# Filling TensorE's waits between attention and the first expert's first product

## The chip, the cores and the metric

The kernel runs on one NeuronCore of a Trainium2 chip. TensorE multiplies, VectorE, ScalarE and GpSimd work on vectors, SyncE (SP) issues most transfers; each engine runs its own instructions in order and waits on semaphores. The time is device microseconds of one execution, given as a median of several; the profile is of one more execution.

## What is computed

Attention over 8 batches, 8 heads, 576 positions and 64 features gives a matrix x of 4608 tokens by 512. Each token then goes to one of eight experts, 576 tokens to each. The reference takes the pairs of token and expert by falling logit, so that the expert that fills first, and with which tokens, comes out of a sorted sweep:

```python
logits = x @ w_gate
order = np.argsort(-logits.flatten())
for idx in order:
    tok, e = (int(idx) // E, int(idx) % E)
    if assigned[tok] >= 0 or counts[e] >= cap:
        continue
    assigned[tok] = e
    counts[e] += 1
for e in range(E):
    mask = assigned == e
    h = np.maximum(x[mask] @ w1[e], 0.0)
    out[mask] = h @ w2[e]
```

## The kernel before

Attention runs in 16 units. A planner (`Plan`) orders each unit's steps on five engines; with the table of due times that the kernel carries, every engine takes its steps in that order. Its PSUM buffers are four, named `g`. The last unit also gives the logits `L`, in the layout of 128 rows by 36 columns of tokens.

Between attention and the experts stands `routing(0)`, the search for the first full expert, written straight in code. A token's best logit is split into six digits. For each digit VectorE compares all tokens with the digit's 32 or 64 values (`cmp`, in pieces), TensorE counts per expert with 36 small products into `rps`, VectorE turns the counts into flags and a sum `da`, one product with `e8s` spreads it, and VectorE takes the digit off (`ch`, `cc`). The first digit's count is mostly made during attention (`part`); what is left of it is 9 products. The first four digits have 32 values and the last two 64 (`fin` is the last). Then come the marks `gt`, a scan and a product with `tri` and `dif` for the rank of each token, two one-hot tables (`hv`, `lo`, the latter compared in three pieces), 18 products, and eight small ones that give the list `idx`: columns 0 to 4 are the rows of the expert's tokens in blocks of 128 (the last of 64), column 5 is an index of half rows, used when the last block is written out.

Idle products, `idle(n)`, of ones with 512 columns into a spare PSUM tile `y1` (PSUM is the accumulator memory), stand at three places: behind the rank product (4), behind `idx` (11), and behind the transposes of the first two blocks (4 and 3).

Tiles of the experts come from a pool `fp`, which takes over SBUF that attention's tiles had. The first instruction of an engine that writes into it waits for all earlier users. `wk` is a one-element copy on GpSimd of a piece of `lo`, in the pool `rt`, which has no earlier users.

The rest of the work is planned as in attention, with a table. What matters here, in the order of each engine for expert 0: GpSimd gathers the five blocks (`xg`), with a copy of the expert's number (`ei`) behind the second one; SP loads the third and fourth piece of the first weight (`raww`) by that copied number; ScalarE splits each weight piece into a high part `w1h`, the residue `w1l` is VectorE's; the gathered blocks are transposed on TensorE into PSUM buffers `h` (four of them) and split the same way into `xh` and `xl`. The products of `xh`, `xl` with the weights (L922) go into the same four buffers; ScalarE's relu gives `fh`, VectorE the residue `fl`, which frees the buffer. ScalarE has the split of the third and fourth weight piece ahead of the first relu. The routing for expert 1 runs in between, on VectorE and TensorE. VectorE's update of the logits for it (L744 to L752) stands behind the last column of `idx`.

Of the kernel before, what the change touches and what calls it, by code (L numbers as in the profile page):

```python
# [97 lines left out]
def attention(ctx, tc, nc, q, k, v, w_phi, w_gate, xs, L, C, xp, cfg={}, after=None, later=None, count=None, init=iter(())):  # L98
# [39 lines left out]
    NG=4  # L138
# [14 lines left out]
    def unit(u):  # L153
# [130 lines left out]
        for g,(j0,j1) in enumerate(JG):  # L284
            n=j1-j0; due=d['num']+d['ns']*g
            js=sorted(set(j//3 for j in range(j0,j1)))
            def pe(x,g=g,j0=j0,j1=j1):
                p=T['np',u,g]=pair(('g',u,'num',g))(x)
                for a in range(2):
                    for j in range(j0,j1):  # L290
                        for fh in range(2):
                            for ab in range(2):
                                PE.matmul(p[64*ab:64*ab+64,a,73*(j-j0):73*(j-j0)+73],T['qP',u,j//3][:,fh,a,ab,j%3,:],T['kz',u][:,a,fh,ab,:],start=fh==0,stop=fh==1)  # L293
            def dve(x,g=g,j0=j0,j1=j1,n=n):
                p=T['np',u,g][:,:,0:73*n].rearrange('p a (j e) -> p a j e',e=73)
                rd=sb.tile([128,2,n,1],F32,name='rd',bufs=2)
                V.tensor_scalar(rd,p[:,:,:,72:73],1e-6,None,op0=OP.add)
                V.reciprocal(rd,rd)
                if g==0: T['x',u]=(xp if lastu else sb).tile([128,9,144],F32,name='xp',bufs=1 if lastu else 2)
                x_=T['x',u]  # L300
                Lb=L[:,9*bp+j0:9*bp+j1,:]
                if lastu:
                    L3=C['L3'][:,j0:j1]
                    for a in range(2): V.tensor_mul(L3[:,:,:,1+a],p[:,a,:,64*a:64*a+8],rd[:,a].to_broadcast([128,n,8]))
                    V.tensor_reduce(Lb.rearrange('p j (e o) -> p j e o',o=1),L3,axis=AX.X,op=OP.add)
                    if g==1: after()
                    for a in range(2):
                        for j in range(n): A.activation(x_[:,j0+j,8+64*a:72+64*a],p[:,a,j,8-8*a:72-8*a],AF.Copy,scale=rd[:,a,j,:])
                else: V.tensor_mul(x_[:,j0:j1].rearrange('p j (a e) -> p a j e',a=2),p[:,:,:,0:72],rd.to_broadcast([128,2,n,72]))
            add(('num',g),'PE',n*515.,due,pe,['zk']+[('ex',j) for j in js],'B',slots(('g',NG,'num',g)),tuple(('qP',u,j) for j in js)+(('kz',u),),ins=32*n)  # L310
            add(('x',g),'DVE',(430+dv(144*n)) if not lastu else 900.,due+2.7,dve,[('num',g)],seq=('x',0) if g else None,slot=slots(('xb',2)) if g==0 else (),frees=(('g',u,'num',g),))
        def st(x):
            for a in range(2):
                o=bass.AP(tensor=xs.tensor,offset=xs.offset+(1152*bp+576*a)*512+128*hp,ap=[[512,64],[64*512,9],[1,128]])
                nc.sync.dma_start(o,T['x',u][64*a:64*a+64,:,8:136])
# [243 lines left out]
def moe(ctx, tc, nc, L, xs, w1, w2, out, C, MC, R0, rt, cfg={}):  # L559
# [18 lines left out]
    def idle(n):  # L578

        p=ps.tile([128,512],F32,name='y1',bufs=1)  # L580
        for _ in range(n): PE.matmul(p,ones,ones[:,None,:].to_broadcast([128,4,128]),start=True,stop=True)
    def routing(r):

        last = r==E-1
        wide = r<cfg.get('wide',1)
        if not last:
# [4 lines left out]
            for i,(sh,bits) in enumerate(DIG):  # L591
                K=KW[i]; n=128//K; fin=i==ND-1
                part='n0' in R and i==0
                if part:
                    p=rps([8,K])
                    cnt0(R,p,NT//9-1,cmp0(R,NT//9-1),True,True)
                else:
                    cmp=S([128,NT//n,K,n],f'cmp{K}',BF,b=2)
                    cv=c.rearrange('p (g i) -> p g i',i=n)
                    g=0  # L600
                    for ck in ((WC if K==32 else WC2) if wide else (9,)*(1 if K==32 else 2)):
                        V.tensor_tensor(cmp[:,g:g+ck],cv[:,g:g+ck,None,:].to_broadcast([128,ck,K,n]),
                                        kt[i].rearrange('p (k i) -> p k i',i=n)[:,None].to_broadcast([128,ck,K,n]),op=OP.is_ge); g+=ck
                if 'rest' in R:
                    with tc.issue_after(R['last']):
                        if i: 
                            for _ in R.pop('rest'): pass
                        else: next(R['rest'])
                yield
                if part: pass  # L610
                elif wide:
                    p=rps([8,K])
                    for t in range(NT):
                        PE.matmul(p,OH[:,t,:],cmp[:,t//n,:,t%n],start=t==0,stop=t==NT-1)
                else:
                    p=rps([128,n,8])
                    for g in range(NT//n):
                        PE.matmul(p,cmp[:,g].rearrange('p k i -> p (k i)'),OH[:,g*n:g*n+n,:],start=g==0,stop=g==NT//n-1)  # L618
                    yield
                    mm=S([128,n,8],f'mm{n}'); V.tensor_mul(mm,p,msk[n])  # L620
                    V.tensor_reduce(tin[:,0:8].rearrange('p (e o) -> p e o',o=1),mm.rearrange('p i e -> p e i'),axis=AX.X,op=OP.add)
                    tr=S([128,32],'tr'); V.transpose(tr,tin)
                    yield
                    cn8=S([128,32//n,1],f'cn{n}'); V.tensor_reduce(cn8,tr.rearrange('p (k i) -> p k i',i=n),axis=AX.X,op=OP.add)
                    f32=S([128,32//n],f'f{n}'); V.tensor_scalar(f32,cn8[:,:,0],float(cap),2.0**(-7*i),op0=OP.is_ge,op1=OP.mult)
                    ds8=S([128,1],'ds'); V.tensor_reduce(ds8,f32,axis=AX.X,op=OP.add)
                if wide:
                    fl=S([8,K],f'fl{K}',BF); da=S([8,1],'da',BF)
                    with nc.allow_low_precision(reason='counts up to 64'):
                        if part: V.scalar_tensor_tensor(fl,p,-float(cap),R['n0'],op0=OP.add,op1=OP.is_ge,accum_out=da)  # L630
                        else: V.tensor_scalar(fl,p,float(cap),0.0,op0=OP.is_ge,op1=OP.add,accum_out=da)
                else:
                    fl=S([128,8],'fl128',BF); V.tensor_scalar(fl,eye8,ds8,None,op0=OP.mult)
                yield
                p=rps([128,8])
                if wide: PE.matmul(p,da.to_broadcast([8,128]),e8s[:,i],start=True,stop=True)
                else: PE.matmul(p,ones,fl,start=True,stop=True)
                if r: yield
                ch=S([128,1],'ch'); V.tensor_reduce(ch,p,axis=AX.X,op=OP.max)
                lat=cfg.get('latd',.7)  # L640
                if fin: break
                c2=S([128,NT],'cc',BF,b=2)
                V.scalar_tensor_tensor(c2,c,ch,dg[:,i+1],op0=OP.subtract,op1=OP.add); c=c2
                if r: yield
# [29 lines left out]
        PE.matmul(p[:,1],dif,gt[:,0],start=False,stop=True)  # L674
        if wide: idle(4)
        if r: yield
# [21 lines left out]
        l2=sf[:,0].rearrange('p (g i) -> p g i',i=2)  # L698
        lk=6 if wide else 9
        for g in range(0,18,lk):  # L700
            V.tensor_tensor(lo[:,g:g+lk],l2[:,g:g+lk,None,:].to_broadcast([128,lk,64,2]),
                            kl.rearrange('p (k i) -> p k i',i=2)[:,None].to_broadcast([128,lk,64,2]),op=OP.is_equal)
        if wide:

            wk=S([1,1],'wk',BF); G.tensor_copy(wk,lo[0:1,0,0,0:1])
        yield
# [5 lines left out]
        if wide:  # L712
# [3 lines left out]
            for j in range(4):  # L716
                for o in (0,64):
                    k=5 if o==0 else 4
                    PE.matmul(p[o:o+64,0:k],dup2[:,j%2,o:o+64],pb[:,o//64:9:2,j//2,j%2],start=j==0,stop=j==3,skip_group_check=True)
            V.tensor_copy(idx[:,0:4,0],p[:,0:4])  # L720
            V.tensor_copy(idx[0:64,4,0:1],p[0:64,4:5])
        else:

# [14 lines left out]
        if not last:  # L738
            yield 'up'
            if wide:  # L740
                p=rps([128,1])
                for j in range(4): PE.matmul(p,dup2[:,j%2],pb[:,8:9,j//2,j%2],start=j==0,stop=j==3)
                V.tensor_scalar(idx[:,5],p,2.0,half,op0=OP.mult,op1=OP.add)
            E1=S([128,8],'E1'); V.tensor_scalar(E1,f8,mx,None,op0=OP.is_equal)  # L744
# [66 lines left out]
    for r in range(E):  # L811
# [132 lines left out]
        for bb,(o,nn) in enumerate(BL):  # L944
# [43 lines left out]
            add(('ys',r,bb),'POOL',1250.,due+d['y']+.5,ys,[('yc',r,bb)],frees=(('ysb',r,bb),)+((('idx',r),) if r else ()),lat=2800.,lock=True)  # L988
    idle(11)
    for x in P.order(): x['fn'](x)  # L990
# [64 lines left out]
```

## Time and profile before

| what | value |
|---|---|
| median of 3 runs | 763.65 us (763.33 to 764.94) |
| the profiled execution | 765.09 us, of which 763.2 us are its span |
| TensorE busy | 736.1 us, 96% of the span |
| VectorE busy | 571.4 us, 75% |
| ScalarE busy | 348.2 us, 46% |
| GpSimd busy | 312.0 us, 41% |
| mean granted TensorE clock | 0.977 of full |

Busy shares are means over stages with different limits, so they do not tell which wait counts; the stretches and timelines below do. In them the first number is the start in us from the beginning of the span. A busy time of several products ends with the tail of the last one. What stands in brackets is the idle time just before on that engine and what ended it. The granted clock is 1.00 at 2.4 GHz and 0.50 at 1.2 GHz.

### The profile page before, as it was taken

To read this page: it belongs to the slowest core of one execution; us is meant where nothing else is said; L and a number is where in the kernel's file an instruction comes from. 1 tells how busy PE (TensorE), PEld (TensorE's weight loads), DVE (VectorE), ACT (ScalarE), POOL (GpSimd) and SP (SyncE) were. 2 spreads that over 40 slices of the span, in tenths; PEclk is the share of its full clock that TensorE was granted. 3 is DMA by queue.
4 is the path that set the end of the run, shared out by engine and by line. 5 is a ranking of instruction groups with operands and counts; after the bars stand their busy time and mean duration, and the time that the engine had idled before them with its cause. 6 is when DMAs were issued, how large, how long until landed. Compare 5 with 4: busy or idle time off the path is not lost.

```text
span 763.2 us, 25319 instructions
## 1 busy us (share of the span) xinstructions
PE 736.1 (96%) x10832; PEld 633.3 (83%) x10832; DVE 571.4 (75%) x1495; ACT 348.2 (46%) x612; POOL 312.0 (41%) x336
## 2 busy tenths in 40 slices
PE   7999999999999966999999999999999999999997
PEld 3888888998898864788897897897897897897985
DVE  5999899989997975996796796796796795673410
ACT  2677677877788431333522422422422422542411
POOL 6797888988889701103103103103103103312002
PEclk9999999999999985999999999999999999999999
DMA  9979688988883032325405405406405406662301
GB/s 168 153 136 154 132 166 165 165 142 156 156 167 81 13 86 75 104 107 186 160 1 182 164 2 183 163 1 186 160 1 184 163 2 198 236 190 60 132 15 49
DMA packets 236944, 94.28 MB, mean 124 GB/s; under 512 B 185904, under 2 KB 223184, under 8 KB 236832
## 3 DMA queue, kind: packets, MB, share of 16 engines
q1 hardware_dynamic: 225552, 71.91, 40.4%
q0 software_dynamic: 6608, 20.16, 8.3%
q8 instruction: 85, 1.39, 0.8%
q10 hardware_dynamic: 4672, 0.59, 0.6%
q14 instruction: 27, 0.22, 0.1%
HBM read 72.58 MB, written 20.05 MB: 121 GB/s over the span
## 4 chain that ended last, share of the span: by engine, by line
PE 65%; issue 13%; DVE 12%; POOL 4%; ACT 2%; SPq 2%; DMA 1%; POOLq 0%; DVEq 0%
PE h L922 22%; PE y L953 18%; PE g L293 8%; DVE kgm L189 4%; PE y L968 3%; PE g L185 3%; PE g L276 2%; PE g L231 2%; SPq L122 2%; DVE qgt L192 2%; DVE qgm L189 2%; PE rps L618 2%; POOL ks L222 1%; PE g L247 1%; PE h L887 1%
## 5 line engine op out<-in xcount | busy, mean ns | idle before, releaser
L983 POOL DMA_INDIRECT out_dram<-ysb,idx x40 | 39.2, 981 | 335.9 <-ACT ysb L976 329.9
L222 POOL TENSOR_TENSOR ks<-ks,kP 128x512 f32<-128x512 f32 x112 | 143.2, 1279 | 7.4 <-ACT kP L213 0.2
L922 PE MATMUL h<-xh,w1l 128*128 128x272 f32 (+3 forms) x512 | 142.0, 297 | 0.3 <-DVE w1l L840 0.2
L922 PE MATMUL h<-xh,w1h 128*128 128x272 f32 (+3 forms) x512 | 141.6, 302 | 0.1
L935 ACT ACTIVATE fh<-h 128x272 fp32r<-128x272 f32 (+2 forms) x128 | 49.1, 384 | 136.6 <-PE h L922 128.8
L953 PE MATMUL y<-w2h,fh 128*128 128x512 f32 x256 | 101.2, 398 | 0.0
L953 PE MATMUL y<-w2l,fh 128*128 128x512 f32 x256 | 99.9, 395 | 0.0
L953 PE MATMUL y<-w2h,fl 128*128 128x512 f32 x256 | 99.3, 392 | 0.0
L922 PEld LDWEIGHTS h<-xh,w1l 128*128 128x128 f32 x512 | 97.1, 190 | 1.8 <-DVE w1l L840 0.8
L922 PEld LDWEIGHTS h<-xh,w1h 128*128 128x128 f32 x512 | 96.0, 190 | 2.0 <-issue 0.4
L922 PE MATMUL h<-xl,w1h 128*128 128x272 f32 (+3 forms) x512 | 93.3, 299 | 1.1 <-DVE xl L897 1.1
L213 ACT ACTIVATE kP<-kgt 128x768 f32<-128x768 f32 x96 | 73.9, 837 | 34.0 <-POOL kgt L201 19.0
L939 DVE SCALAR_TENSOR_TENSOR fl<-h,fh 128x272 fp32r<-128x272 f32 (+2 forms) x128 | 53.0, 416 | 38.7 <-ACT fh L935 22.2
L293 PE MATMUL g<-kz,qP 128*64 128x73 f32 x2304 | 78.9, 229 | 2.0 <-DVE kz L262 1.8
L293 PEld LDWEIGHTS g<-kz,qP 128*64 128x64 f32 x2304 | 76.3, 138 | 3.8 <-DVE kz L262 1.9
L280 ACT ACTIVATE qP<-g 128x768 f32<-128x768 f32 x96 | 70.9, 813 | 16.1 <-PE g L276 16.1
L922 PEld LDWEIGHTS h<-xl,w1h 128*128 128x128 f32 x512 | 76.5, 190 | 1.8 <-DVE xl L897 1.3
L231 PE MATMUL g<-kP,vi 64*64 64x256 f32 x1152 | 70.5, 377 | 0.1
L976 ACT COPY ysb<-y 128x512 f32<-128x512 f32 (+1 forms) x40 | 21.8, 546 | 100.5 <-issue 59.2
L953 PEld LDWEIGHTS y<-w2l,fh 128*128 128x128 f32 x256 | 48.2, 188 | 9.0
L953 PEld LDWEIGHTS y<-w2h,fl 128*128 128x128 f32 x256 | 48.2, 188 | 8.8
L953 PEld LDWEIGHTS y<-w2h,fh 128*128 128x128 f32 x256 | 48.3, 189 | 8.3
(220 smaller groups left out, 1314.7 us busy)
## 6 DMA issues: line engine op xcount, KB each, us to landing
raww<-in_moe_w_dram SPq DMA_DIRECT2D x64, 512.0 KB, 5.2
xs<-xp SPq DMA_DIRECT2D x32, 288.0 KB, 4.7
ki<-in_k_dram SPq DMA_DIRECT2D x62, 144.0 KB, 3.9
qi<-in_q_dram SPq DMA_DIRECT2D x62, 144.0 KB, 4.0
vi<-in_v_dram SPq DMA_DIRECT2D x56, 144.0 KB, 4.1
vi<-in_v_dram POOLq DMA_DIRECT2D x8, 144.0 KB, 7.2
xl<-xd SPq DMA_DIRECT2D x4, 288.0 KB, 4.3
xd<-xg SPq DMA_DIRECT2D x4, 256.0 KB, 3.5
```

Of the source, the lines that this page charges most:

```text
L185: PE.matmul(p[64*bi:64*bi+64,a,128*(s-s0):128*(s-s0)+128],t[r,bi,s,:],C['w'][r,:],start=True,stop=True)
L189: V.tensor_reduce(m,vw(),axis=AX.X,op=OP.max,apply_absolute_value=True)
L213: for i in range(2): A.activation(o[:,:,:,128*i:128*i+128],t,AF.Exp,scale=1.0-2*i)
L222: else: G.tensor_add(ks,ks,kP[:,s])
L231: PE.matmul(p[64*a:64*a+64,i,0:256],v_[r,a,s,:],kP[r,s,a,:],start=s==0,stop=s==8,skip_group_check=True)
L280: for fh in range(2): A.activation(t[:,fh].rearrange('p i a s t -> p i (a s t)'),p,AF.Exp,scale=1.0-2*fh)
L293: PE.matmul(p[64*ab:64*ab+64,a,73*(j-j0):73*(j-j0)+73],T['qP',u,j//3][:,fh,a,ab,j%3,:],T['kz',u][:,a,fh,ab,:],start=fh==0,stop=fh==1)
L922: PE.matmul(p,ws[:,k,o:o+128],xx[:,k,o1:o2],start=n==0,stop=n==11)
L935: A.activation(hh[:,f,o1:o1+m1],p[:,0:m1],AF.Relu)
L939: V.scalar_tensor_tensor(hl[:,f,o1:o1+m1],p[:,0:m1],0.0,hh[:,f,o1:o1+m1],op0=OP.max,op1=OP.subtract)
L953: PE.matmul(p,hx[:,f,o:o+128],ws[:,f%2,:],start=n==0,stop=n==23)
L983: st=G.indirect_dma_start(out=ov,out_offset=bass.IndirectOffsetOnAxis(ap=iv,axis=0),in_=yv,in_offset=None)
```

## The change

Six things are edited, all around `routing(0)`:

- Eleven idle products of 512 columns run at the end of attention's last unit, as a step of the plan behind its last product (`warm`).
- A new `fill(n)` gives n idle products of 256 columns into the same spare tile: 6 behind the first digit's count, 1 behind each further count, 7 behind each spreading product, 12 behind the last one. `idle(4)` behind the ranks becomes `idle(11)`.
- `lo` is compared in pieces of 7, 7 and 4 groups instead of 6, 6, 6.
- `wk` is taken from the pool `fp`, and a new one-element memset on VectorE, `wv`, also from `fp`, stands behind the compares of the fourth digit.
- Column 5 of `idx` is computed right behind the others, ahead of the long run of idle products and ahead of VectorE's update of the logits.
- That run, `idle(11)`, becomes `idle(20)`.

```diff
+        if lastu:
+            def wm(x):
+                p=pair(('g',u,'warm'))(x)
+                for _ in range(11): PE.matmul(p[:,0],w[:,0:128],w,start=True,stop=True)
+            P.add(('warm',u),'PE',2400.,1e6,wm,[(('num',1),u)],lat=0.,mode='W',slot=(('g',NG,('g',u,'warm')),),frees=(('g',u,'warm'),),ins=11)
...
+    def fill(n):
+
+        p=ps.tile([128,512],F32,name='y1',bufs=1)[:,0:256]
+        for _ in range(n): PE.matmul(p,ones,ones[:,None,:].to_broadcast([128,2,128]),start=True,stop=True)
...
+                if wide and i==3: V.memset(fp.tile([1,1],BF,name='wv',bufs=1),0.0)
...
-                if part: pass
+                if part: fill(6)
                 elif wide:
                     p=rps([8,K])
                     for t in range(NT):
                         PE.matmul(p,OH[:,t,:],cmp[:,t//n,:,t%n],start=t==0,stop=t==NT-1)
+                    fill(1)
...
-                if wide: PE.matmul(p,da.to_broadcast([8,128]),e8s[:,i],start=True,stop=True)
+                if wide:
+                    PE.matmul(p,da.to_broadcast([8,128]),e8s[:,i],start=True,stop=True)
+                    fill(12 if fin else 7)
...
-        if wide: idle(4)
+        if wide: idle(11)
...
-        lk=6 if wide else 9
-        for g in range(0,18,lk):
+        g0=0
+        for lk in (7,7,4) if wide else (9,9):
+            g=g0; g0+=lk
...
-            wk=S([1,1],'wk',BF); G.tensor_copy(wk,lo[0:1,0,0,0:1])
+            wk=fp.tile([1,1],BF,name='wk',bufs=1); G.tensor_copy(wk,lo[0:1,0,0,0:1])
...
+            p5=rps([128,1])
+            for j in range(4): PE.matmul(p5,dup2[:,j%2],pb[:,8:9,j//2,j%2],start=j==0,stop=j==3)
             V.tensor_copy(idx[:,0:4,0],p[:,0:4])
             V.tensor_copy(idx[0:64,4,0:1],p[0:64,4:5])
+            V.tensor_scalar(idx[:,5],p5,2.0,half,op0=OP.mult,op1=OP.add)
...
-            if wide:
-                p=rps([128,1])
-                for j in range(4): PE.matmul(p,dup2[:,j%2],pb[:,8:9,j//2,j%2],start=j==0,stop=j==3)
-                V.tensor_scalar(idx[:,5],p,2.0,half,op0=OP.mult,op1=OP.add)
...
-    idle(11)
+    idle(20)
```

How the instructions stand, first on TensorE, between the count of the fourth digit and that of the fifth. Before, the spreading product (`da`) follows the last of the 36 counting products (`OH`), and the next count follows it:

```order
L614 LDWEIGHTS OH
L614 MATMUL rps<-cmp_5977,OH 8x32
L636 LDWEIGHTS da [waits DVE_49]
L636 MATMUL rps<-e8s,da 128x8
L614 LDWEIGHTS OH
L614 MATMUL rps<-cmp_6028,OH 8x64 [waits DVE_49]
```

In the change the same place begins so (`onesb` is the tile of ones):

```order
L624 LDWEIGHTS OH
L624 MATMUL rps<-cmp_6024,OH 8x32
L590 LDWEIGHTS onesb
L590 MATMUL y_6068<-onesb 128x256 [waits PE_49]
L648 LDWEIGHTS da [waits DVE_49]
L648 MATMUL rps<-e8s,da 128x8
L590 LDWEIGHTS onesb
L590 MATMUL y_6075<-onesb 128x256 [waits PE_49]
L590 LDWEIGHTS onesb
L590 MATMUL y_6075<-onesb 128x256
```

One idle product has come in ahead of the spreading product and seven behind it, of which two are shown; the next count stands behind them.

On GpSimd, the place is the copy `wk` and the gathers. Each name in a list of waits is one semaphore: those with DMA are of transfer queues. Before:

```order
L705 COPY wk<-cmp_6181 1x1 [waits DVE_49]
L852 DMA xg<-xs,idx 128x512 [waits DMASW7_49,DMASW6_49,DMAHW0_49,DMASW5_49,DMAHW1_49,DMASW4_49,DMAHW2_49,DMASW3_49,DMAHW3_49,DMASW2_49,DMAHW4_49,DMASW1_49,DMAHW5_49,DMASW0_49,DMAHW6_49,DVE_49,DMAHW7_49,Activation_49,Pool_49]
L852 DMA xg<-xs,idx 128x512
L818 COPY ei_6264<-ei 128x1
L852 DMA xg<-xs,idx 128x512 x2
```

And in the change:

```order
L719 COPY wk<-cmp_6272 1x1 [waits DMASW6_49,DMASW7_49,DMASW5_49,DMAHW0_49,DMASW4_49,DMAHW1_49,DMASW3_49,DMAHW2_49,DMASW2_49,DMAHW3_49,DMASW1_49,DMAHW4_49,DMASW0_49,DMAHW5_49,DVE_49,DMAHW6_49,PE_49,DMAHW7_49,Activation_49,Pool_49]
L865 DMA xg<-xs,idx 128x512 [waits DMAHW7_49,DMAHW6_49,DVE_49]
L865 DMA xg<-xs,idx 128x512
L831 COPY ei_6364<-ei 128x1
L865 DMA xg<-xs,idx 128x512 x2
```

The long list of waits has moved from the first gather to the copy ahead of it; the gather keeps three.

On VectorE, the place is the list `idx` and, behind the update of the logits, the first weight residue `w1l`. Before:

```order
L721 CAST idx<-rps 64x1
L743 TENSOR_SCALAR idx<-rps,half 128x1 [waits PE_49]
L744 TENSOR_SCALAR E_6238<-f_6130,mx 128x8
L746 TENSOR_TENSOR g_6241<-gt 128x36
L747 SCALAR_TENSOR_TENSOR mem<-si,g_6241 128x36 [waits DVE_49]
L748 TENSOR_TENSOR un<-un,mem 128x36 [waits DVE_49]
L749 TENSOR_TENSOR opn<-opn,E_6238 128x8
L751 TENSOR_TENSOR sc<-mem,E_6238 128x288
L752 SCALAR_TENSOR_TENSOR L<-sc,L 128x288 [waits DVE_49]
L840 TENSOR_TENSOR w1l_6250<-raww_6152,w1h_6249 128x512 [waits DMASW7_49,DMAHW0_49,DMASW6_49,DMAHW2_49,DMASW5_49,DMAHW3_49,DMASW4_49,DMAHW4_49,DMASW3_49,DMAHW5_49,DMASW2_49,DMAHW6_49,DMASW1_49,DMAHW7_49,DMASW0_49,Activation_49]
```

And in the change:

```order
L737 CAST idx<-rps 64x1
L738 TENSOR_SCALAR idx<-rps,half 128x1 [waits PE_49]
L757 TENSOR_SCALAR E_6338<-f_6214,mx 128x8
L759 TENSOR_TENSOR g_6341<-gt 128x36
L760 SCALAR_TENSOR_TENSOR mem<-si,g_6341 128x36 [waits DVE_49]
L761 TENSOR_TENSOR un<-un,mem 128x36 [waits DVE_49]
L762 TENSOR_TENSOR opn<-opn,E_6338 128x8
L764 TENSOR_TENSOR sc<-mem,E_6338 128x288
L765 SCALAR_TENSOR_TENSOR L<-sc,L 128x288 [waits DVE_49]
L853 TENSOR_TENSOR w1l_6350<-raww_6236,w1h_6349 128x512 [waits DMAHW0_49,Activation_49]
```

The weight residue keeps two waits. Column 5 of `idx` (`128x1`) has the same neighbours as before, but the product that it waits for now stands ahead of the idle products on TensorE. The other waits stand on the memset, behind the compares of the fourth digit in the change:

```order
L611 TENSOR_TENSOR cmp_6024<-cc,kt_189 128x128 [waits DVE_49]
L611 TENSOR_TENSOR cmp_6024<-cc,kt_189 128x256
L611 TENSOR_TENSOR cmp_6024<-cc,kt_189 128x384 x2
L613 MEMSET wv 1x1 [waits DMASW7_49,DMASW6_49,DMAHW2_49,DMASW5_49,DMAHW3_49,DMASW4_49,DMAHW4_49,DMASW3_49,DMAHW5_49,DMASW2_49,DMAHW6_49,DMASW1_49,DMAHW7_49,DMASW0_49,Pool_49]
L642 TENSOR_SCALAR fl_6070,da<-rps 8x32 [waits PE_49]
```

The memset is the only row that is new there.

## Rows read from the trace of the kernel before

**Rows 1.** Stages: stretch, its length, busy time of each engine, clock, DMA.
```profile
360.00:750.00 390.00, 390.00 (x2974) 339.22 (x2973) 262.56 (x826) 134.51 (x290) 69.30 (x103) 1.00 0.36 119
```

**Rows 2.** Stages, TensorE alone: length, busy (count), granted clock, DMA, GB/s.
```profile
280.50:304.30 23.80, 15.90 (x214) 0.50 0.23 70
...
311.20:314.50 3.30, 3.30 (x18) 0.50 0.14 48
```

**Rows 3.** Timeline of TensorE, 277 to 307: start, us, line, operation [wait].
```profile
277.78 0.71 PE L514 MATMUL rps<-cmp,OH 128*8 128x32 bf16 x9 [2.73 <-DVE s L458]
278.85 0.17 PE L636 MATMUL rps<-e8s,da 8*128 8x8 bf16 x1 [0.36 <-DVE fl L630]
279.83 1.37 PE L614 MATMUL rps<-cmp,OH 128*8 128x32 bf16 x36 [0.81 <-DVE cmp L602]
...
282.48 1.38 PE L614 MATMUL rps<-cmp,OH 128*8 128x32 bf16 x36 [0.81 <-DVE cmp L602]
...
287.99 2.08 PE L614 MATMUL rps<-cmp,OH 128*8 128x64 bf16 x36 [1.01 <-DVE cmp L602]
...
295.61 0.22 PE L673 MATMUL rps<-gt,tri 128*128 128x72 bf16 x1 [1.45 <-DVE gt L657]
...
298.39 1.29 PE L709 MATMUL rps<-hv,cmp 128*128 128x36 bf16 x18 [0.83 <-DVE cmp L701]
...
300.28 4.51 PE L581 MATMUL y<-onesb 128*128 128x512 bf16 x11
...
305.47 1.03 PE L581 MATMUL y<-onesb 128*128 128x512 bf16 x4
```

**Rows 4.** Timeline of VectorE, 282 to 308.
```profile
282.20 0.96 DVE L602 TENSOR_TENSOR cmp<-cc,kt 128x128 bf16<-128x128 bf16 x4
...
287.51 1.63 DVE L602 TENSOR_TENSOR cmp<-cc,kt 128x512 bf16<-128x512 bf16 x5
...
300.38 0.16 DVE L720 CAST idx<-rps 128x4 int32<-128x4 f32 x1 [0.47 <-PE rps L719]
...
304.91 0.22 DVE L743 TENSOR_SCALAR idx<-rps,half 128x1 int32<-128x1 f32 x1 [4.30 <-PE rps L742]
...
307.13 0.69 DVE L840 TENSOR_TENSOR w1l<-raww,w1h 128x512 fp32r<-128x512 f32 x1 [0.31 <-issue]
```

**Rows 5.** Timeline of GpSimd, 301 to 307.
```profile
301.47 1.06 POOL L852 DMA_INDIRECT xg<-xs,idx  x1 [2.63 <-DMA raww<-in_moe_w_dram]
...
303.81 0.19 POOL L818 COPY ei<-ei 128x1 int32<-128x1 int32 x1
...
305.44 0.95 POOL L852 DMA_INDIRECT xg<-xs,idx  x1 [0.30 <-issue]
```

**Rows 6.** Timelines of ScalarE and GpSimd, a later block's way out.
```profile
365.79 0.59 ACT L976 COPY ysb<-y 128x512 f32<-128x512 f32 x1
...
366.65 0.98 POOL L983 DMA_INDIRECT out_dram<-ysb,idx  x1 [3.04 <-ACT ysb L976]
```

**Rows 7.** Timeline of ScalarE, 313 to 315.
```profile
313.37 1.04 ACT L837 CAST w1h<-raww 128x1024 fp32r<-128x1024 f32 x1 [2.09 <-DMA raww<-in_moe_w_dram]
314.32 0.65 ACT L935 ACTIVATE fh<-h 128x256 fp32r<-128x256 f32 x2
```

**Rows 8.** Timeline of VectorE, 314 to 318.
```profile
314.74 0.76 DVE L939 SCALAR_TENSOR_TENSOR fl<-h,fh 128x256 fp32r<-128x256 f32 x2 [0.16 <-ACT fh L935]
...
316.26 0.19 DVE L620 TENSOR_TENSOR mm<-rps,msk 128x32 f32<-128x32 f32 x1 [0.17 <-PE rps L618]
...
317.78 0.23 DVE L633 TENSOR_SCALAR fl<-eye,ds 128x8 bf16<-128x8 f32 x1
```

**Rows 9.** Timeline of TensorE, 310 to 319.
```profile
310.88 1.04 PE L922 MATMUL h<-xl,w1h 128*128 128x256 f32 x4 [1.06 <-DVE xl L897]
...
316.95 0.71 PE L887 MATMUL h<-ident,xg 64*128 64x64 f32 x16
...
318.06 0.17 PE L637 MATMUL rps<-fl,onesb 128*128 128x8 bf16 x1
```

## Prediction

> **What bounds the kernel now.** I read the busy time and granted clock by stage first, then the timelines of the engines around the change, and last the rows just behind it, to see what a gain must get past. From 360 to 750 us TensorE is busy in all 390.00 us [rows 1]: whatever starts the experts earlier ends the kernel earlier, unless a wait behind the change eats it. From 280.5 to 304.3 us the granted clock was 0.50, which is 1.2 of 2.4 GHz, and TensorE was busy 15.90 of 23.80 us [rows 2]; before it fell, TensorE had waited 2.73 us for the last block's marks [rows 3]. That stretch is the routing of the first expert: VectorE compares, TensorE counts, six times over, each waiting for the other. After it come gather, transposes and first products. The reader should see three things there. A count of 36 products takes 1.38 us with 32 columns and 2.08 us with 64 [rows 3]. The eleven idle products hold TensorE 4.51 us [rows 3], and VectorE waits 4.30 us behind them for the last index [rows 4]. The first gather starts at 301.47, although its indices are there at 300.38 + 0.16 = 300.54 [rows 4, 5].
>
> **The counts.** At 1.2 GHz 36 products of 32 columns need 1.38 us; 64 columns at 2.4 GHz are the same work per clock, so at most 2.08 - 1.38 = 0.70 us is won in each of the two 64-column digits. VectorE's compares limit that: they end at 287.51 + 1.63 = 289.14 [rows 4], the count at 290.07, so 0.93 us later. In the 32-column digit the compares end at 282.20 + 0.96 = 283.16 and the count at 283.86, 0.70 later, with 12 of 36 products left behind the last compare. Behind the last compare of a 64-column digit there are only 4, so 8 x 1.38/36 = 0.31 less remains: 0.39. The saving is 0.23 (0.93 - 0.70) to 0.54 (0.93 - 0.39) a digit; I take 0.52, since the piece left is really the short one: **1.04 us** for two, bounds 0 (clock stays low) and 1.40. The 32-column digits win nothing: the one at 279.83, mostly ahead of the fall, took 1.37, the one at 282.48 behind it 1.38.
>
> **The fills.** Four 512-column products took 1.03 us in the high state, the last one's tail included, so one is under 0.26; eleven took 4.51 us nearly all in the low state, so 0.41 there and half of it, 0.21, at the double clock [rows 3]. I take 0.22, and 0.11 for 256 columns. Seven (0.77) go into a hole of 0.81, in the two long digits 1.01; twelve (1.32) into 1.45; eleven long ones ahead (11 x 0.22 = 2.42) into 2.73 [rows 3]. All fit, by 0.04 to 0.31 us, so they cost nothing while the clock is high. The six behind the first count (0.66) do not fit: that hole is 0.36 us [rows 3] plus the tail of the count. I charge 0.10, bounds 0 and 0.30 (0.66 - 0.36). The seven added to the four behind the ranks make 2.42 us, where before four at the low clock (4 x 0.41 = 1.64) and a wait of 0.83 stood, 2.47 [rows 3]; they just fit. The 7, 7, 4 split leaves two groups less behind the last compare; the rows don't resolve it and I leave it out. So the indices come **0.94 us** earlier.
>
> **The waits.** The order shows the first gather with some twenty waits before, and three after; the rest stand on the one-element copy ahead of it, which runs while GpSimd has nothing to do. The gather started 301.47 - 300.54 = 0.93 us behind its indices. A later indirect transfer that has its own wait as the last thing starts 366.65 - (365.79 + 0.59) = 0.27 us behind its source [rows 6]. So 0.93 - 0.27 = **0.66 us** is won, bounds 0 and 0.66; the lower end holds if the wait was truly for the weight transfer that its row names, since the copy ahead would then wait for that in the gather's place. VectorE's memset takes up fifteen waits; before, they held the first weight residue 0.31 us [rows 4]. They now lie in VectorE's wait for the fourth count, which is as long as for any 32-column count (0.70), so they cost nothing there; uncovered they would cost those 0.31.
>
> **The last index** no longer queues behind the idle products, so VectorE's update of the logits (304.91 to 306.82, 1.91 us) runs from about 299.7 instead, beside the gather's flight. VectorE is then free when the weights' and tokens' residues are due, and TensorE's wait of 1.06 us for the token residue [rows 9] should go. Twenty idle products instead of eleven stand ahead of the first transposes: 20 x 0.22 = 4.40 us from about 299.4, to 303.8, where eleven slow ones ended at 300.28 + 4.51 = 304.79; what they hold up is covered by the slack below.
>
> **What is late next.** Not VectorE, but weights. GpSimd's copy of the expert's number (303.81) follows the second gather, SP's load of the third and fourth weight piece follows that copy [rows 5], and ScalarE splits the fourth piece only at 313.37, when it has landed [rows 7]. Behind that split, in ScalarE's queue, stand the first two relus (314.32, 0.65), then VectorE's residues of them (314.74, 0.76), which free the two PSUM buffers that the next transposes need. These ran at 316.95, later than 315.50, when the buffers were free: slack 1.45 us. But VectorE goes on without a hole from 314.74, but for 0.17 us for a count, to 317.78 + 0.23 = 318.01, and TensorE's next routing product runs at 318.06, directly on it [rows 8, 9]. So the stream of products that lasts to the end moves with the landing of the fourth weight piece. That follows the gather: 0.94 + 0.66 = 1.60 us, and the 0.17 us wait goes too, since TensorE now comes early. It does come early enough: from 310.88 to 316.95 it worked 6.07 us, 3.30 of them at half clock [rows 2, 9], so 4.4 at full clock; it must start by 313.9 - 4.4 = 309.5, and the gather's move alone brings 310.88 to 309.3.
>
> **Sum:** 1.04 - 0.10 + 0.66 + 0.17 = 1.77 us. The profiled execution took 765.09 us (span 763.2 and 1.9 around it), which would become 763.3; it lies 1.44 us above the median of 763.65 of the runs shown, so in such runs **761.9 us**.
>
> **Rivals.**
> *The clock falls in the new waits (R1).* TensorE, now early, waits for the buffers until about 313.9 and again for the routing product until 316.3, with under 1.1 us of work between. In the profile the clock fell after a wait of 1.06 us and a shorter one: at 311.2 to 314.5 it was 0.50 [rows 2]. There it cost nothing, since VectorE was later anyway. A like stretch of 3.3 us from 316 on would cost up to 1.65 us, some 1.0 in the mean: 762.9. For it speaks that the waits are longer than those; against it, that where the low stretch begins may differ from run to run. The Trainium skill (TensorE: Matmul & The Clock Gate, What's actually happening) states just that: the same kernel showed 6, 11 or 14 products at the low clock at its start, and the page warns against fitting a count. By it the loss would lie anywhere from 0 to 1.65 us, and in before too; the one profile here cannot show it.
> *More is won (R2).* The fourth piece's landing is late in a queue that it shares with three gathers; if it comes another 1.2 us earlier, TensorE can follow, since VectorE, done with the update at 301.6, no longer makes it wait at 310.88: 760.7. No row says that it would.
> *The fills are late (R3, slower).* If the clock is low in the routing in spite of them, a 512-column product costs 0.41 us and one of 256 columns 0.21. Seven are then 1.47 us in holes of 0.81 (three) and 1.01 (two), so 2.9 late in all, six 0.9 (1.26 - 0.36), twelve 1.1 (2.52 - 1.45), eleven long ones 2.0 (4.51 - 2.47): 6.9 us, less 0.83 that the waits give back: 769.7. If only the last two groups meet the low clock, 3.1 - 0.83 - 0.5 (one long digit is saved): 765.4. It decides from the point where the clock is low at the fourth digit. Against it: with the fills the holes of 0.81 to 1.45 us are nearly shut, and it was behind a hole of 2.73 that the clock fell.
> *The gather does not start earlier than its indices allowed (R4).* Its wait is replaced by another: VectorE's update now runs beside the first two gathers. The Trainium skill (SBUF — State Buffer, Who interferes with whom) says that VectorE in some modes and GpSimd lock a port pair against each other, and the later one waits. By it the gathers could lose up to the update's 1.91 us. The rows speak against it: a gather beside that same update took 0.95 us, the first one, beside an idle VectorE, more [rows 5]. With the 0.66 gone the time is 762.5; with all of 1.91 lost, 763.8.
>
> **Chances.** Forecast 0.47, R1 0.24, R2 0.12, R3 0.08, R4 0.09. A run can tell 0.2%, 1.5 us, from no change here. The forecast's own range is 761.2 to 762.6, a fifth of it above the mark of 762.1; R2 is beyond it; R1 and R4 are the same; R3 slower. So faster 0.38 + 0.12 = 0.50, same 0.42, slower 0.08. The range leaves out R3 and the far half of R2: 760.4 to 764.0.
>
> **What would show it.** Right: granted clock 1.00 from 275 us to the first product, 64-column counts of about 1.5 us, the first gather 0.3 us behind its indices, the update of the logits directly behind the last index, ScalarE's fourth split near 311.7, and TensorE waiting for the transposes. Wrong: a clock of 0.50 anywhere between 280 and 300, counts that start behind fills, a gather of over 1.1 us, or a fourth split that has not moved with the gather.

## The result, and the profile after

The changed kernel takes **769.94 us** in the median of nine runs (765.33 to 773.0), the kernel before 764.65 us beside it (762.15 to 766.01): ratio 1.007, 95% interval 1.0046 to 1.0094. It is slower by about 5.3 us, where 761.9 was forecast. The profiled execution took 772.88 us with a span of 770.8, against 765.09 and 763.2.

The first thing to look at is not the stage that was edited but where it begins. Attention's last work on VectorE before the routing is the reduction L305. Timeline of VectorE, first of the kernel before, then of the changed one:

```profile
275.86 0.25 DVE L305 TENSOR_REDUCE L<-L 128x32 f32<-128x96 f32 x1
```

```profile
283.99 0.25 DVE L305 TENSOR_REDUCE L<-L 128x32 f32<-128x96 f32 x1
```

Attention ends 8.13 us later. Of the instructions edited only the eleven idle products at its end have begun by then, and the delay is there ahead of them: TensorE's last product of attention ends at 283.18, where it ended at 275.05 in the kernel before. So all rows behind it have to be read from this mark (275.86 before, 283.99 after). A single execution places it to within a few microseconds only: 273.8 to 279.4 in all profiles of kernels with attention's tiles in good places, below, and 282.6 to 284.0 in those with bad ones. Timeline of TensorE in the changed kernel, rows that answer to [rows 3, 9]:

```profile
285.90 0.71 PE L519 MATMUL rps<-cmp,OH 128*8 128x32 bf16 x9 [0.24 <-DVE s L463]
286.54 0.83 PE L590 MATMUL y<-onesb 128*128 128x256 bf16 x6
287.30 0.17 PE L648 MATMUL rps<-e8s,da 8*128 8x8 bf16 x1
...
296.42 1.52 PE L624 MATMUL rps<-cmp,OH 128*8 128x64 bf16 x36
...
307.47 4.48 PE L586 MATMUL y<-onesb 128*128 128x512 bf16 x20
...
321.30 1.04 PE L900 MATMUL h<-ident,xg 64*128 64x64 f32 x16 [1.07 <-DVE fl L952]
...
323.88 0.17 PE L650 MATMUL rps<-fl,onesb 128*128 128x8 bf16 x1 [1.00 <-DVE fl L644]
...
330.82 0.18 PE L650 MATMUL rps<-fl,onesb 128*128 128x8 bf16 x1
```

Stages of the changed kernel, TensorE alone (length, busy and count, granted clock, DMA, GB/s); they answer to [rows 2]:

```profile
288.60:312.40 23.80, 22.37 (x294) 1.00 0.28 83
323.70:330.30 6.60, 6.42 (x38) 0.51 0.00 0
```

The fills do what they are for: the clock stays at 1.00 in the routing, and a 64-column count takes 1.52 us instead of 2.08. Later, from 323.7 to 330.3, it is at its lower level; it fell behind a wait of 1.07 us and within one of 1.00. Timelines of VectorE, GpSimd and ScalarE in the changed kernel, for [rows 4, 5, 7]:

```profile
307.46 0.16 DVE L736 CAST idx<-rps 128x4 int32<-128x4 f32 x1 [0.39 <-PE rps L733]
307.54 0.14 DVE L737 CAST idx<-rps 64x1 int32<-64x1 f32 x1
...
307.79 0.22 DVE L757 TENSOR_SCALAR E<-f,mx 128x8 f32<-128x8 f32 x1
```

```profile
307.91 1.07 POOL L865 DMA_INDIRECT xg<-xs,idx  x1 [1.68 <-DVE idx L737]
```

```profile
319.45 1.05 ACT L850 CAST w1h<-raww 128x1024 fp32r<-128x1024 f32 x1 [1.48 <-DMA raww<-in_moe_w_dram]
320.41 0.93 ACT L948 ACTIVATE fh<-h 128x256 fp32r<-128x256 f32 x3
```

The gather starts 307.91 - 307.68 = 0.23 us behind the last index it needs (0.93 before), and it names `idx` as what it waited for.

Counted from attention's end, each step by the first start of its row (the rows of expert 1's routing, L637 before and L650 after, are the "routing products"); the two middle columns are experiments of the section below:

| us from attention's end | before | products alone | waits alone | changed |
|---|---|---|---|---|
| indices | 24.52 | 23.52 | 24.46 | 23.47 |
| first gather | 25.61 | 24.60 | 24.91 | 23.92 |
| fourth split | 37.51 | 35.84 | 35.89 | 35.46 |
| first routing product | 42.20 | 40.59 | 40.31 | 39.89 |
| second routing product | 47.08 | 45.46 | 45.19 | 46.83 |
| end of the span | 487.3 | 485.7 | 485.4 | 486.8 |

In every column the first routing product stands 4.42 to 4.75 us behind the fourth split: it moves with the landing of that weight piece, as the prediction had it. So the edited stage gained 42.20 - 39.89 = 2.31 us in this profile, the low clock took 2.06 of them back (6.94 us between the two routing products instead of 4.88), and 0.5 us were left at the end. The 7.6 us by which the span is longer are 8.13 lost in attention less those 0.5.

**Where attention loses.** The views of the DMA queues for the first 45 us (packets, MB, share of the 16 engines' time), kernel before and changed kernel:

```profile
q1 hardware_dynamic: 35081, 4.73, 69.9%
...
q10 hardware_dynamic: 4672, 0.59, 9.4%
```

```profile
q1 hardware_dynamic: 31721, 4.30, 87.2%
...
q10 hardware_dynamic: 4672, 0.59, 14.0%
```

q10 is the cleanest, since it carries hardly anything but 128-byte pieces of k and q, where q1 has v's 256-byte pieces among them. The same 4,672 packets (ScalarE's four loads of 144 KB, 1,152 pieces each, are 4,608 of them) take 9.4% of 16 x 45 us, 14.5 ns each, before, and 14.0%, 21.6 ns, after. q1 moves less data in more time: 14.3 and 19.8 ns a packet. At TensorE this ends in a wait (row of before, then of after), with VectorE's rows of after below it:

```profile
26.23 0.59 PE L276 MATMUL g<-ident,qgt 64*128 64x64 f32 x12
```

```profile
29.95 0.90 PE L276 MATMUL g<-ident,qgt 64*128 64x64 f32 x12 [4.32 <-DVE qgt L192]
```

```profile
28.19 0.78 DVE L174 STREAM_TRANSPOSE kT<-ki 128x576 f32<-128x576 f32 x1 [5.05 <-DMA ki<-in_k_dram]
28.89 0.92 DVE L192 TENSOR_TENSOR qgt<-g,qgm 128x768 f32<-128x768 f32 x1
```

TensorE waits 4.32 us for `qgt`, which stands in VectorE's queue behind the transpose of a k tile whose landing VectorE awaited for 5.05 us. By 100 us TensorE has done 154 products less (x2100 and x1946 in the stage from 17 us; busy time of the engines, then clock, DMA, GB/s):

```profile
17.00:100.00 83.00, 79.29 (x2100) 68.59 (x2100) 76.06 (x114) 57.20 (x79) 69.65 (x63) 0.96 0.85 147
```

```profile
17.00:100.00 83.00, 75.36 (x1946) 65.64 (x1950) 69.90 (x106) 52.98 (x73) 64.77 (x59) 0.92 1.01 141
```

The order of attention's instructions is the same in both kernels. What differs is where its tiles lie in SBUF. The one-element tile `wk` took a slot of 32 bytes in the routing's pool, and the change moved it to the experts' pool; attention's pool follows the routing's, so all its tiles moved down by 32 bytes. The programs as built place the first tiles, in bytes of a partition, at:

```
                 before             changed
ki          61696 = 241 x 256   61664 = 240 x 256 + 224
qi          70912 = 277 x 256   70880 = 276 x 256 + 224
vi         138592 = 541 x 256 + 96   138560 = 541 x 256 + 64
```

k and q are loaded in pieces of 128 bytes (32 elements; the innermost step of the access pattern in `raw`), 36 behind each other in a partition:

```python
o=bass.AP(tensor=x.tensor,offset=x.offset+((2*bp+a)*H+2*hp)*HS+32*db,ap=[[D,32],[32*D,36],[1,32]])
```

Before, none of these pieces crosses a multiple of 256 bytes; in the changed kernel every second one does. v comes in pieces of 256 bytes, and each of those crosses one in both kernels.

### The profile page after: what moved, and what is told of

Read it like the earlier page. It is cut to its first block, busy times and chain, and to the rows that moved or that the text cites. A ratio compares the mean times of both kernels' runs of the same rounds, so it can differ in the third digit from the quotient of the medians.

```text
span 770.8 us, 25492 instructions
## 1 busy us (share of the span) xinstructions
PE 749.2 (97%) x10917; PEld 644.4 (84%) x10917; DVE 572.4 (74%) x1496; ACT 348.2 (45%) x612; POOL 312.8 (41%) x336
## 3 DMA queue, kind: packets, MB, share of 16 engines
q10 hardware_dynamic: 4672, 0.59, 0.8%
## 4 chain that ended last, share of the span: by engine, by line
PE 70%; issue 12%; DVE 7%; DMA 3%; SPq 3%; POOL 2%; ACT 1%; POOLq 0%; DVEq 0%
PE h L935 21%; PE y L966 18%; PE g L293 9%; PE g L185 5%; PE g L231 4%; PE y L981 3%; SPq L122 3%; PE g L276 3%; DVE kgm L189 2%; PE rps L629 1%; PE g L247 1%; DVE qgt L192 1%; DMA ki<-in_k_dram 1%; PE g L260 1%; PE h L900 1%
## 5 line engine op out<-in xcount | busy, mean ns | idle before, releaser
L293 PEld LDWEIGHTS g<-kz,qP 128*64 128x64 f32 x2304 | 76.5, 138 | 4.2 <-DVE kz L262 1.9
```

## Experiments

Each kernel is compared with the kernel before in runs taken beside it, whose medians were 764.83 to 765.13 us; across experiments the ratios compare better than the times.

**Theory A: placement.** Theory B, its rival in the texts below, is that the products themselves, or spread, delay attention. Attention's tiles are put back, in the first kernel alone and in the second with the experts' tiles, which the change had moved up by 32 bytes. The first edit, against the changed kernel:

```diff
-                if wide and i==3: V.memset(fp.tile([1,1],BF,name='wv',bufs=1),0.0)
+                if wide and i==3: V.memset(fp.tile([1,128],BF,name='wv',bufs=1)[:,0:1],0.0)
...
             wk=fp.tile([1,1],BF,name='wk',bufs=1); G.tensor_copy(wk,lo[0:1,0,0,0:1])
+            S([1,1],'gap',BF)
```

> The changed kernel with one unused 32-byte tile in the routing's pool, which puts attention's tiles back at the addresses of the kernel before (the change had moved them down by 32 bytes, since the one-element tile wk left that pool); the expert pool keeps the places of the change but for a whole 256 bytes. Theory A (placement): the 128-byte pieces of k and q that land 32 bytes lower take longer, and that alone is the 8.1 us by which attention ended later; then attention ends near 284 - 8 = 276 us of the span, the first 45 us show q1 at about 70% of the DMA engines as before and not 87%, and the time is 761.5 to 764.5 us, ratio to before 0.996 to 1.000. Theory B (the products themselves, a longer program of TensorE, or the chip's own spread): the place doesn't matter, attention ends near 283 us as in the changed kernel, and the time stays at 767 to 773 us.

Measured: 764.58 us, ratio 0.9992 (0.9973 to 1.0011); 0.1 us above the range expected, its ratio inside; attention ends at 276.98, q1 at 70.2% and q10 at 9.8%. In the second, `wk` too is 256 bytes wide:

> As the kernel with attention's tiles put back, and with the expert pool's tiles too at the place within 256 bytes that they had before (the two one-element tiles made 256 bytes wide). Theory A with weights: the loads of the first weights and the stores of the experts matter as well, and this is 0.5 to 1.5 us faster than the kernel with attention alone put back. Theory A without them: within 0.5 us of it, 761.5 to 764 us. Theory B: 767 to 773 us.

Measured: **762.95 us, ratio 0.9971 (0.9955 to 0.9986)**; attention ends at 276.09, q1 at 70.9% and q10 at 9.7%. Theory B falls with both: the same products and waits, with tiles in the old places, cost attention nothing. With all placement mended the change is faster than the kernel before by 0.29%, 2.2 us; with attention's tiles alone put back no gain is clear of noise.

Now the other way round, the kernel before with tiles moved and nothing else:

```diff
             wk=S([1,1],'wk',BF); G.tensor_copy(wk,lo[0:1,0,0,0:1])
+            S([1,112],'gap',BF)
...
     fp=ctx.enter_context(tc.tile_pool(name='ffn',bufs=2))
+    fp.tile([1,16],BF,name='gap2',bufs=1)
```

> The kernel before, with nothing changed but an unused tile of 224 bytes in the routing's pool and one of 32 bytes ahead of the experts' tiles: attention's tiles stand 224 bytes higher, at the same place within 256 bytes as in the changed kernel, and the experts' tiles a whole 256 bytes higher. Theory A: attention ends 6 to 8 us later, q1 takes about 87% of the first 45 us, and the time is 770 to 773 us. Theory B: 764 to 765 us, as before.

Measured: 773.12 us, ratio 1.0104 (1.0079 to 1.013); attention ends at 282.59, 6.73 us later than in the kernel before. With 64 bytes (`gap` of 32 elements, `gap2` of 96):

> The kernel before with attention's tiles 64 bytes higher and the experts' a whole 256 higher. It tells two forms of theory A apart. If every second 128-byte piece that crosses a 256-byte boundary of its partition is what costs, 64 costs as much as 224: 769 to 773 us. If pieces cost that do not begin at a multiple of 64 bytes, 64 costs nothing: 764 to 765 us. Theory B: 764 to 765 us.

Measured: 772.15 us, ratio 1.0085 (1.006 to 1.0109); attention ends at 282.85. With 128 bytes:

> The kernel before with attention's tiles 128 bytes higher and the experts' a whole 256 higher. k's and q's 128-byte pieces then begin at 128 and at 0 of a 256-byte stretch by turns, so that none crosses a boundary, though the tiles no longer begin at a multiple of 256. If the crossing is what costs, the time is that of the kernel before, 764 to 766 us, with q1 near 70% in the first 45 us and attention's end near 276 us. If any place other than a multiple of 256 costs, 769 to 773 us, as with 64 and 224 bytes.

Measured: 766.6 us, 0.6 above the range expected, ratio 1.0015 (0.9999 to 1.0032); attention ends at 275.12. The queues of the three in the first 45 us, for 224, 64 and 128 bytes:

```profile
q1 hardware_dynamic: 30604, 4.16, 89.3%
...
q10 hardware_dynamic: 4672, 0.59, 14.0%
```

```profile
q1 hardware_dynamic: 31606, 4.28, 79.6%
...
q10 hardware_dynamic: 4672, 0.59, 13.6%
```

```profile
q1 hardware_dynamic: 35072, 4.72, 70.9%
...
q10 hardware_dynamic: 4672, 0.59, 9.3%
```

A packet of q1 takes 21.0, 18.1 and 14.6 ns (14.3 in the kernel before). Neither the distance from the old place counts nor a multiple of 64 bytes: 128 costs at most the little that is left open below, and 64 and 224, where every second piece crosses a multiple of 256, cost 7 to 8 us. These places cannot tell that rule from another, that a piece has to begin at a multiple of 128: with pieces of 128 bytes both name the same places. The median with 128 bytes is 1.5 us above the kernel before, with an interval that reaches down to 0.9999; its profiled execution shows nothing of it, so whether some small cost is left there stays open.

The Trainium skill (DMA: Bandwidth & Descriptors, How a descriptor splits into AXI transactions) has a rule for this: transactions of 256 bytes that start at multiples of 256, in beats of 32 bytes, with the bytes ahead of the start fetched for nothing. The page states it for what a transfer reads; here it is the written side that moved. An estimate by that rule for two neighbouring pieces of 128 bytes: 12 beats at 0 and at 128, 18 at 224, 16 at 64, that is 1.00, 1.00, 1.50 and 1.33. In q1's packets the trace shows 1.00 (kernel before), 1.01, 1.46 and 1.26. In q10's it shows 1.00, 0.99, 1.49 and 1.45: there 64 costs as much as 224, which beats don't give. v speaks against beats too: by the same estimate a 256-byte piece is 11 beats at 96 and 15 at 224, but from 45 to 255 us q1 took 77.0% in the kernel before (v at 96) and 77.4% in the one with 128 bytes (v at 224). So the runs bear out that the place within 256 bytes matters, and not the price by beats.

Do the experts' tiles matter in the same way? The kernel before with `fp.tile([1,1],BF,name='gap2',bufs=1)` behind `wk`:

> The kernel before with the experts' tiles from the fifth 4096-byte one on 32 bytes higher, where the changed kernel has them, and attention's tiles in their old places. The kernel with only attention's tiles put back took 764.58 us and the one with all put back 762.95, so if the experts' places are worth that difference, this takes 766 to 767.5 us, ratio 1.001 to 1.003. If that difference was spread between runs, 764.5 to 765.3 us, ratio 0.999 to 1.001.

Measured: 765.23 us, ratio 0.9997 (0.9978 to 1.0016). No effect is seen, though this profile has attention's end at 279.38 (it is of the slowest of its twelve runs); so the 1.6 us between the first two experiments, whose intervals overlap, are not explained by the experts' tiles. The runs' mean granted clocks give a hint: 0.993 or less in six of the first kernel's twelve runs and in four of the second's.

**The edits one by one,** with attention's and the experts' tiles in good places. The kernel before with the added products only (the fills, the eleven at attention's end, 11 and 20 for 4 and 11):

```diff
-                if part: pass
+                if part: fill(6)
...
+                    fill(12 if fin else 7)
...
-        if wide: idle(4)
+        if wide: idle(11)
```

> The kernel before with nothing but the products that compute nothing: eleven at attention's end, the fills in the count stage, 11 and 20 in place of 4 and 11 later; lists and waits as before, and all tiles in their old places. By the prediction's terms the two 64-column counts give back 1.04 us and fill(6) costs 0.10, so the first gather starts 24.7 us behind attention's end (25.6 before) and the time is 763.5 to 764.5 us, ratio 0.9980 to 0.9995. The rival is that the longer program of TensorE costs something by itself: then 766 us or more with attention ending later than 276 us.

Measured: 764.98 us, ratio 0.9984 (0.9969 to 0.9999); its median is above the range expected and not below the 764.83 us of the kernel before beside it, its ratio is inside. So a gain in time is barely shown. The gather starts 24.60 us behind attention's end, expected 24.7. Attention ends at 277.92, 2 us later than in the profile of the kernel before, and at 277.76 in the next kernel, which has none of the products; so this is spread, not the products. And the lists and waits without the products; the edit is shown against the changed kernel, for the products alone:

```diff
-                if part: fill(6)
+                if part: pass
...
-                    fill(12 if fin else 7)
...
-        if wide: idle(11)
+        if wide: idle(4)
```

> The mended list and waits alone (the first gather's wait moved to the copy wk, the sixth index column made ahead of the idle products, one-hot pieces of 7, 7 and 4), without any of the added products, all tiles at the aligned places. By the prediction's terms the clock is 0.50 in the routing as before, the gather starts 0.66 us earlier (24.95 us behind attention's end), the index update 0.17, and the time is 763.5 to 764.5 us, ratio 0.9985 to 1.0000. If the products and the waits each give their own term, the gains of this kernel and of the one with the products alone add up to the 2.2 us of the two together.

Measured: 764.01 us, ratio 0.9985 (0.9971 to 1.0). The gather starts 24.91 us behind attention's end, expected 24.95, with the clock at 0.50. The two gains, 0.16% and 0.15%, add up to 0.31%, and together they gave 0.29%; but each has an interval of some 0.15% to either side, so that they add up is not more than compatible with this. Timelines of GpSimd, products alone and waits alone; the wait of the first is still 2.50 us long, with its start 302.52 - 301.66 = 0.86 us behind the index, while the second needs 302.67 - 302.44 = 0.23:

```profile
302.52 1.06 POOL L864 DMA_INDIRECT xg<-xs,idx  x1 [2.50 <-DVE idx L733]
```

```profile
302.67 1.07 POOL L859 DMA_INDIRECT xg<-xs,idx  x1 [1.80 <-DVE idx L731]
```

**The late fall of the clock.** Idle products in TensorE's wait ahead of the 64-row transposes, all tiles in place as in the second experiment:

```diff
+                if r==0 and two: idle(5)
                 p=[ps.tile([128,4,128],F32,name='h%d'%y['buf'][('xp',r,b0,i)],bufs=1) for i in range(2 if two else 1)]
```

> The changed kernel with all tiles aligned, and five more idle products on TensorE ahead of the first expert's 64-row transposes, where it waits 0.5 to 1.3 us for VectorE's residues (1.07 us in the changed kernel, with the clock at 0.50 for the next 6.8 us). If that wait is what lets the clock fall there and the fall costs some 2 us where it happens, no run shows it any more: granted clock 0.994 or more in most runs, and a median 0.5 to 1.5 us below the 762.95 us without them, 761.5 to 762.5 us. If the fall has another cause, 763 us as without them, or more by the length of the five products (1.1 us) where TensorE did not wait.

Measured: 762.74 us, ratio 0.9971 (0.9958 to 0.9983). From 275 to 760 us the clock was 1.00 in its profile, but so it was in that of the kernel without these products, and the medians are 0.2 us apart. Nor do the runs show it gone: four of twelve have a mean granted clock of 0.993 or less here (762.4 to 764.4 us, the other eight 762.2 in the mean), as without the products (764.2 to 765.2 us, the others 762.1). So these products are not shown to help; where in those runs the low clock lay is not on record.

**Better than both.** If pieces that cross a multiple of 256 cost, v's 256-byte pieces cost in all kernels so far: they begin at 96 in the kernel before and at 64 in the changed one. 160 bytes ahead of them, which also move the tiles behind, mend it:

```diff
+        if u==0: sb.tile([128,40],F32,name='gapv',bufs=1)
         t=T['v',u]=sb.tile([128,2,9,D],F32,name='vi',bufs=2)
```

> The changed kernel with all tiles aligned, and 160 unused bytes ahead of v's tiles, which began 96 bytes behind a multiple of 256 in all kernels so far: now each of v's 256-byte pieces lies inside one 256-byte stretch. If the placement theory holds for v as for k and q, v's pieces take 2 to 5 ns less of their 18 to 20, attention's start is shorter by 0.3 to 1.5 us, and the time is 761.5 to 762.7 us. If the loads of v are hidden anyway, 762.5 to 763.5 us, as without.

Measured: 761.77 us, ratio 0.9961 (0.9947 to 0.9975). From 45 to 255 us q1's packets took 73.5% of the engines' time, against 77.5% with v at 96 (76.5 to 77.9 in all eight profiles with k and q in good places and v not), and attention ended at 273.81, the earliest of all. The median is 1.2 us lower, but the intervals overlap. With the five idle products as well:

> The changed kernel with all tiles aligned, v's too, and the five idle products ahead of the 64-row transposes. If v's places are worth 1.2 us as the one run with them says (761.77 against 762.95 us) and the five products nothing (762.74), this takes 761.3 to 762.2 us, ratio 0.9955 to 0.9970; if the low median of the kernel with v aligned was spread, 762.5 to 763 us.

Measured: **760.32 us, ratio 0.9921 (0.9898 to 0.9943)**, the fastest of all, 4.7 us below the kernel before (765.05 beside it; the two medians alone give 0.9938). It lies below both ranges expected and is more than the two effects measured apart. q1 took 74.0% from 45 to 255 us, so that v's places relieve the queue is seen twice; but attention ended at 276.44, no earlier than with v at 96. A candidate for the rest is the late low clock, which some runs have and others don't; that it makes up the difference is not shown.

## Why the prediction was wrong

**The step that failed** is the base of the sum: "The profiled execution took 765.09 us ..., which would become 763.3". It takes all that runs ahead of the edits as unchanged. The move of `wk` was costed as a wait only; it is also 32 bytes of SBUF, and those cost some 5 to 8 us: 8.0 (773.12 - 765.13) when made alone, 5.4 (769.94 - 764.58) when undone for attention's tiles alone, 7.0 (769.94 - 762.95) when undone for all. No rival had it. The 2.2 us that the edits do give are less than that. A smaller part of the base is spread: it was brought to a median of three runs, 763.65 us, and the nine beside the result gave 764.65.

**The counts: right.** Forecast 1.04 us for the two long digits; a count takes 1.52 us instead of 2.08, and from compare to compare such a digit takes 3.02 us where it took 3.59, 0.57 each, 1.14 together.

**The fills: one of them mis-sized.** All groups but one fit. The six behind the first count cost 0.32 and not 0.10, with an upper bound of 0.30: the product L648 comes 3.31 us behind attention's end, L636 came 2.99 behind it. The indices still came 24.52 - 23.47 = 1.05 us earlier (forecast 0.94), because of a gain that the sum did not have: from the start of the last count to the indices it took 8.02 us instead of 8.80, 0.21 more than that count's own 0.57. That the two nearly cancel is luck.

**The waits: right.** Forecast 0.66 for the gather; it moved 25.61 - 23.92 = 1.69 us, 0.64 more than the indices. VectorE's update of the logits stands directly behind the last index (307.79).

**What is late next: right in kind.** TensorE does wait for the buffers `h` (1.07 us, for VectorE's residue) and again for expert 1's routing product, which follows the fourth split by 4.43 us instead of 4.69 (forecast 0.17 less). The fourth split moved 2.05 us where 1.60 was forecast, and the routing product 2.31 instead of 1.77, so part of R2 came with it. Why the weight piece lands earlier than the gather's move gives is not settled: in four kernels with the same instructions up to that split and all tiles in good places it stood 33.57, 34.20, 34.87 and 35.18 us behind attention's end.

**R1 came true in the changed kernel's profile,** larger than priced: 6.8 us at the low level instead of 3.3, 2.06 us lost where some 1.0 was expected in the mean and 1.65 at most. In the kernel with attention's tiles alone put back, a wait of 1.34 us was followed by ten microseconds at 0.50 (one of 0.28 lies in them); in the one with v aligned, waits of 0.48 and 1.00 us by none; in the one with all aligned there was 0.55 us of waiting, and no fall. So in these kernels it comes in some executions and not in others, and what it costs in the mean is not shown. **R3** is refuted: the clock was 1.00, and no count started behind a fill; of the spreading products only the first did. That its 769.7 us is close to the 769.94 measured is chance. **R4** did not show: the first gather lost nothing to VectorE's update, 1.07 us against 1.06.

With the placement mended, 762.95 us lies 2.2 us under the kernel before, where 1.77 was forecast. That is near, but in part by luck, for R1 and R2 pull against each other. The profile of the kernel with all tiles in place shows what R2 described, and more of it (another 2.3 us instead of 1.2): its fourth split (first row) stands 33.57 us behind attention's end and the routing product (second row) 38.00, 4.2 us earlier than before.

```profile
309.66 1.05 ACT L851 CAST w1h<-raww 128x1024 fp32r<-128x1024 f32 x1 [0.44 <-DMA raww<-in_moe_w_dram]
```

```profile
314.09 0.17 PE L650 MATMUL rps<-fl,onesb 128*128 128x8 bf16 x1 [0.55 <-DVE fl L644]
```

From attention's end to the end of the span it took 483.1 us, and 483.7 to 484.8 in the three later kernels built on it, none with a low clock there; the changed kernel and the one with attention's tiles alone put back, both with a late fall of the clock, took 486.8 and 488.0. The kernel before took 487.3, and 486.3 to 487.3 in all profiles of its instructions. So the path of the prediction held, and the base did not; the 2.2 us are probably a mean of executions that gain more and of others that lose it again, which single profiles suggest and don't show.

## What to carry to other kernels

A tile moved between pools moves every tile behind it. Where transfers land in pieces of 128 or 256 bytes, compare the tiles' places within 256 bytes before and after an edit, and pad: an unused tile of 32 bytes was worth 5.4 us here, more than all the work on waits. When a change moves the time, first find where the stage it touches begins; a shift that is already there by then was not caused in that stage. And look for the same fault in the kernel before: 160 bytes ahead of v's tiles lowered the queue's share in both kernels that had them, and the median by 1.2 us in one comparison and by 2.4 in the other, the first of them within the noise.

## What had not been expected of the hardware

Loads of 128-byte pieces (q10, first 45 us) took 14.3 to 14.5 ns a packet in the kernel before and with its tiles 128 bytes higher, where no piece crosses a multiple of 256 bytes of its partition, and 21.0 to 21.6 with tiles 64 or 224 bytes higher, where every second one does; no instruction differed in order or form. This kernel, whose start waits for such loads, took 7 to 8 us longer for it.
